# Turning and spreading k's column maxima on VectorE instead of TensorE, for twenty of thirty-two units

## The chip, the cores and the metric

The kernel runs on one core of a Trainium2 chip. A core has a matrix engine (TensorE, PE in the profile; its weight loads are PEld), VectorE (DVE), ScalarE (ACT), GpSimd (POOL), and SyncE (SP), which here issues most of the DMAs. Each engine works through its own queue in order; engines wait for one another by semaphores. On-chip memory is SBUF and, for the results of TensorE, PSUM; both have 128 partitions. The metric is the device time of one execution in microseconds, as the median of several.

## What is computed

An attention without a score matrix, and a mixing network behind it. All inputs are fp32:

```python
def _attn_ref(q, k, v):  # each (8, 8, 576, 64)
    q_s = q - np.max(q, axis=-1, keepdims=True)
    q_s = np.exp(q_s)
    q_s = q_s / (np.sum(q_s, axis=-1, keepdims=True) + 1e-09)
    k_s = k - np.max(k, axis=2, keepdims=True)
    k_s = np.exp(k_s)
    k_s = k_s / (np.sum(k_s, axis=2, keepdims=True) + 1e-09)
    kv = np.einsum('bhsd,bhse->bhde', k_s, v)
    return np.einsum('bhsd,bhde->bhse', q_s, kv)
...
    xt = x.transpose(0, 2, 1)  # x: the heads joined, (8, 576, 512)
    h = np.maximum(xt @ w_tok1, 0.0) @ w_tok2
    u = x + h.transpose(0, 2, 1)
    h2 = np.maximum(u @ w_ch1, 0.0) @ w_ch2
    return u + h2
```

The part that matters here is the softmax of k: it runs over the sequence (axis 2), so each of the 64 columns of a head has one maximum over 576 rows.

## The kernel before

The work on the attention is cut into 32 **units**, each a batch entry and a pair of heads: 128 columns (two heads of 64), 576 rows in five blocks of 128 (the last 64 rows stand twice, which changes no maximum). The network behind it is cut into nine **groups** of 512 rows. A group has twelve **steps**; a step is `ch1` (line 402: twelve matmuls of 512 columns into one PSUM bank `ps_h`, then a rectifier that splits the result into a high part `h2h` on ScalarE, line 412, and a low part `h2l` on VectorE, line 413) and, one step later, `ch2` (line 417: twelve matmuls that add to the four banks `ps_o`, line 421). The products use fp32r operands in pairs of high and low parts; a few small products use plain fp32. After a group's last step `out_end` (line 438) adds the input to the output on VectorE (lines 452 and 453) and stores it.

The first eight units (`early`) are worked before the steps begin. Units 8 to 31 are woven into the steps by the list `todo` (lines 551 to 583): units 8 to 11 two steps apart, units 12 to 31 three steps apart. For a unit n from 12 on come at its step `stage_kv(n)` (the product of k and v, line 277), `stage_y(n)`, `stage_qT(n)` and `soft(n + 1)`, then the loads of unit n + 2, `stage_h1(n)` and, at the next unit, `stage_u(n)`. This is the order in which the program is written; the order in each engine's queue is laid out by Tile when the program is built (line 666), which moves an instruction ahead where its inputs are ready. So an instruction of one unit may run some units ahead.

`soft(n)` is `softmax_k` (line 216) and `softmax_q` (line 240). Both k and its transpose `kt` are loaded, so that the maxima can be had by a reduce along the free axis: line 219 reduces `kt` (128 columns on the partitions, 640 rows along the free axis, 64 of them twice) to `mc`, one number for each partition. But k itself lies with the rows on the partitions and the columns along the free axis, so the 128 maxima must be turned from a column into a row, and the row must be on all partitions. For the units from the ninth on this goes in three steps: ScalarE multiplies the identity by `mc` into `dg`, a diagonal matrix (line 233); TensorE multiplies a matrix of ones by it, which puts the row of the maxima on every partition of a PSUM bank (line 235); ScalarE copies that to `mb` in SBUF (line 236). GpSimd subtracts `mb` from k (line 237), ScalarE takes the exponential (line 238), and a later `stage_kv` reads it.

`dg` and `mb` are one buffer each, for all units; `mc` has two; `kt` has one and k two. `ps_unit` (line 119) hands out the PSUM banks of `ps_h` in turn, four of them, shared with `ch1`.

`stage_qT` (line 296) turns q on VectorE in a similar way to what the change does: a transpose of 32x32 blocks (line 315), then copies of the blocks to their places (line 323), two of three on VectorE and one on ScalarE. GpSimd's other operation in a unit is the low part of q, line 115, in `split`.

Of the kernel before, what the change touches and what calls it, by code (L numbers as in the profile page):

```python
# [8 lines left out]
F32 = mybir.dt.float32  # L9
F32R = mybir.dt.float32r  # L10
U32 = mybir.dt.uint32
AF = mybir.ActivationFunctionType
# [3 lines left out]
P = 128  # L16
# [4 lines left out]
def attn_mixer_kernel(ctx: ExitStack, tc: tile.TileContext, q, k, kt, v, wt, out, dims):  # L21
# [3 lines left out]
    nc = tc.nc  # L25
    B, H, S, D, TOK, DM, DCH, wide = dims
    NJ = DM // P
# [8 lines left out]
    NE = 2 * NJ  # L36
# [6 lines left out]
    sm = ctx.enter_context(tc.tile_pool(name="sm", bufs=2))  # L43
# [6 lines left out]
    ident = const.tile([P, P], F32R, name="ident")  # L50
# [11 lines left out]
    ones = const.tile([P, P], F32, name="ones")  # L62
# [26 lines left out]
    dg = lay.tile([P, P], F32, name="dg")  # L89
    for i in range(3):  # L90
        slots[i][1] = lay.tile([P, NJ, CW], F32R, name=f"ul{i}")
    mb = lay.tile([P, P], F32, name="mb")
# [14 lines left out]
    Q = 32  # L107

    def f32(ap):
        return ap.bitcast(F32)  # L110
# [8 lines left out]
    def ps_unit(dtype=F32):  # L119

        pools = unit_banks[0]
        pool, name = pools[turn[0] % len(pools)]
        turn[0] += 1
        return pool.tile([P, 512], dtype, name=name)
# [90 lines left out]

    def softmax_k(u):
        ktt = u["kt"]
        mc = sm.tile([P, 1], F32, name="mc")
        nc.vector.tensor_reduce(mc, ktt, axis=AX.X, op=ALU.max)  # L219
        kx = u["k"]  # L220
        if u["early"]:
            nc.vector.tensor_scalar(mc, mc, -1.0, None, op0=ALU.mult)
            nc.scalar.activation(ktt, ktt, AF.Exp, bias=mc)
            t = ps_unit()
            for c in range(C):
                nc.tensor.transpose(t[:, c * P : (c + 1) * P], ktt[:, c * P : (c + 1) * P], f32(ident))
            nc.scalar.copy(kx[:, 0:C, :], t.rearrange("p (c d) -> p c d", c=C))
            t = ps_unit()
            turned_k.append(nc.tensor.transpose(t[:, 0:P], ktt[:, S0 : S0 + P], f32(ident)).ins)
            nc.scalar.copy(kx[:, C, :], t[:, 0:P])  # L230
            return

        nc.scalar.activation(dg, f32(ident), AF.Copy, scale=mc)  # L233
        t = ps_unit()
        nc.tensor.matmul(t[:, 0:P], ones, dg, start=True, stop=True)  # L235
        nc.scalar.copy(mb, t[:, 0:P])  # L236
        nc.gpsimd.tensor_tensor(kx, kx, mb.unsqueeze(1).broadcast_to([P, C1, P]), op=ALU.subtract)  # L237
        nc.scalar.activation(kx, kx, AF.Exp)

# [223 lines left out]
    def soft(n):  # L463
        if n < NU:
            softmax_k(units[n])
            softmax_q(units[n])
# [204 lines left out]
```

## Time and profile before

| | us |
|---|---|
| median of three runs | 818.27 (816.95 to 819.36) |
| the profiled execution | 817.88 |
| its span, from the first to the last instruction | 816.1 |
| TensorE busy in the span | 797.1 |
| VectorE busy | 486.7 |
| ScalarE busy | 342.2 |
| GpSimd busy | 83.6 |
| line 235, TensorE busy, 48 matmuls in 24 units | 9.4 |
| mean TensorE clock granted | 0.992 of full speed |

How to read the rows that follow. A row of a group has the line, the engine, the operation, what it writes and reads, the shape of one and the number of them; behind the first bar the busy time in all and the mean of one in ns; behind the second the idle time of the engine just before them, and what ended it. A row of the timeline has the start, the time from the first start to the last end of the instructions merged in it, and the instruction; a bracket shows idle time of the engine before it and its releaser. A row of the windows has the stretch, its length, and for each engine the busy time with the number of instructions. Matmuls overlap: the one behind starts before the one ahead has ended, so their cost is read from start to start.

### The profile page before, as it was taken

The numbers are of one execution on the slowest core, as the hardware profiler recorded it, in microseconds if no ns is written. First come the engines' busy times: TensorE is split into PE (matmuls) and PEld (weight loads), VectorE is DVE, ScalarE is ACT, GpSimd is POOL, SyncE is SP. The second block draws the span as 40 slices with busy tenths as digits, with TensorE's granted clock in tenths as the row PEclk, the third lists the DMA queues.
The fourth block names the chain that finished last, engine by engine and source line by source line (L and its number), as shares of the span: only waits on it lengthen the run. The fifth ranks groups of instructions, "written<-read, shape, count | busy, mean of one in ns | idle before, by whom it ended". The sixth has DMA issues, their size and how long they took to land.

```text
span 816.1 us, 11997 instructions
## 1 busy us (share of the span) xinstructions
PE 797.1 (98%) x4512; PEld 677.0 (83%) x4512; DVE 486.7 (60%) x1104; ACT 342.2 (42%) x898; POOL 83.6 (10%) x69
## 2 busy tenths in 40 slices
PE   7799999989999999999999999999999999999997
PEld 5688888878888888888888888888888888888886
DVE  6999998887876555755576555755575314113112
ACT  6977564448553334343444444443443321101110
POOL 1000010102121100111111111111011100000200
PEclk8999999999999999999999999999999999999999
DMA  9752433414223111322232222312121001001001
GB/s 298 245 162 93 149 110 109 145 65 124 86 63 115 52 30 53 110 61 64 63 100 79 64 64 63 113 51 63 26 87 35 15 1 51 1 1 52 1 1 51
DMA packets 60633, 63.55 MB, mean 78 GB/s; under 512 B 40864, under 2 KB 40992, under 8 KB 60576
## 3 DMA queue, kind: packets, MB, share of 16 engines
q1 hardware_dynamic: 55392, 53.36, 21.8%
q10 hardware_dynamic: 5184, 9.44, 3.1%
q8 instruction: 35, 0.57, 0.3%
q14 instruction: 22, 0.18, 0.1%
HBM read 53.35 MB, written 9.44 MB: 77 GB/s over the span
## 4 chain that ended last, share of the span: by engine, by line
PE 89%; DVE 6%; DMA 3%; ACT 1%; issue 1%; DVEq 0%; ACTq 0%
PE ps_h L409 34%; PE ps_o L421 34%; PE ps_h L381 8%; PE ps_h L337 6%; PE ps_h L277 2%; DMA stg<-in_w 2%; PE ps_h L345 1%; PE ps_o L381 1%; DVE mc L219 1%; PE ps_h L235 1%; DVE cv_s L176 1%; DVE q_t L323 1%; DMA q_t<-in_q 1%; DVE st L245 1%; ACT q_t L251 1%
## 5 line engine op out<-in xcount | busy, mean ns | idle before, releaser
L409 PE MATMUL ps_h<-uh,cw 128*128 128x512 f32 x864 | 269.7, 392 | 0.6 <-DVE cw L115 0.6
L421 PE MATMUL ps_o<-h2h,cw 128*128 128x512 f32 x864 | 263.4, 394 | 2.2 <-DVE cw L115 2.2
L421 PEld LDWEIGHTS ps_o<-h2h,cw 128*128 128x128 f32 x864 | 160.6, 189 | 34.3 <-ACT h2h L412 2.4
L409 PEld LDWEIGHTS ps_h<-uh,cw 128*128 128x128 f32 x864 | 160.3, 188 | 33.2 <-DVE cw L115 1.0
L412 ACT ACTIVATE h2h<-ps_h 128x512 fp32r<-128x512 f32 x108 | 64.5, 597 | 292.8 <-PE ps_h L409 276.6
L413 DVE SCALAR_TENSOR_TENSOR h2l<-ps_h,h2h 128x512 fp32r<-128x512 f32 x108 | 74.0, 685 | 187.3 <-ACT h2h L412 186.9
L409 PE MATMUL ps_h<-ul,cw 128*128 128x512 f32 x432 | 168.2, 389 | 0.0
L421 PE MATMUL ps_o<-h2l,cw 128*128 128x512 f32 x432 | 161.7, 392 | 0.0
L421 PEld LDWEIGHTS ps_o<-h2l,cw 128*128 128x128 f32 x432 | 81.4, 189 | 16.8
L409 PEld LDWEIGHTS ps_h<-ul,cw 128*128 128x128 f32 x432 | 81.1, 188 | 17.0
L115 POOL TENSOR_TENSOR ql<-q_t,qh 128x640 fp32r<-128x640 f32 x24 | 39.3, 1636 | 484.8 <-ACT qh L114 406.3
L323 DVE COPY q_t<-cv_s 32x160 f32<-32x160 f32 (+1 forms) x264 | 65.8, 249 | 6.3 <-POOL ql L115 3.0
L245 DVE TENSOR_REDUCE st<-q_t 128x10 f32<-128x640 f32 x32 | 26.2, 818 | 41.8 <-DMA q_t<-in_q 41.8
L237 POOL TENSOR_TENSOR k_t<-k_t,mb 128x640 f32<-128x640 f32 x24 | 38.0, 1582 | 73.8 <-ACT mb L236 73.8
L323 ACT COPY q_t<-cv_s 32x128 f32<-32x128 f32 (+1 forms) x120 | 36.8, 307 | 2.1 <-DVE cv_s L315 0.7
L219 DVE TENSOR_REDUCE mc<-kt_t 128x1 f32<-128x640 f32 x32 | 26.0, 812 | 14.7 <-ACT dg L233 12.4
L381 PE MATMUL ps_h<-w2h,hh 128*128 128x320 f32 (+1 forms) x112 | 33.4, 299 | 0.0
L256 ACT ACTIVATE q_t<-q_t 128x640 f32<-128x640 f32 x24 | 17.8, 741 | 36.4 <-DVE q_t L255 36.4
L381 PE MATMUL ps_h<-w2l,hh 128*128 128x320 f32 (+1 forms) x112 | 33.0, 296 | 0.0
L381 PE MATMUL ps_h<-w2h,hl 128*128 128x320 f32 (+1 forms) x112 | 32.7, 298 | 0.0
L388 ACT CAST uh<-ps_h 128x320 fp32r<-128x320 f32 (+4 forms) x76 | 25.4, 336 | 15.1 <-PE ps_h L381 11.8
L389 DVE TENSOR_TENSOR ul<-ps_h,uh 128x320 fp32r<-128x320 f32 (+4 forms) x76 | 27.2, 373 | 4.0 <-ACT uh L388 3.1
(144 smaller groups left out, 1061.9 us busy)
## 6 DMA issues: line engine op xcount, KB each, us to landing
stg<-in_w SPq DMA_DIRECT2D x28, 512.0 KB, 4.1
kt_t<-in_kt SPq DMA_DIRECT2D x32, 320.0 KB, 3.1
q_t<-in_q SPq DMA_DIRECT2D x32, 320.0 KB, 3.3
v_t<-in_v SPq DMA_DIRECT2D x64, 128.0 KB, 2.8
out<-stg ACTq DMA_DIRECT2D x32, 256.0 KB, 2.1
k_t<-in_k SPq DMA_DIRECT2D x24, 320.0 KB, 3.5
v_t<-in_v SPq DMA_DIRECT2D x32, 32.0 KB, 2.7
out<-part ACTq DMA_DIRECT2D x4, 256.0 KB, 2.0
```

What stands on the lines that cost most here:

```text
L115: lo_eng.tensor_tensor(lo, src, f32(hi), op=ALU.subtract)
L219: nc.vector.tensor_reduce(mc, ktt, axis=AX.X, op=ALU.max)
L237: nc.gpsimd.tensor_tensor(kx, kx, mb.unsqueeze(1).broadcast_to([P, C1, P]), op=ALU.subtract)
L245: nc.vector.tensor_reduce(st[:, 0, :], qt, axis=AX.X, op=ALU.max)
L323: eng(qx[ys, 0:n, xs], turned[xs, 0:n, ys])
L337: nc.tensor.matmul(y[:, 0:TOK], a, w, start=(i == 0), stop=(i == len(mm) - 1))
L381: nc.tensor.matmul(t[:, 0:N], a, w, start=(i == 0), stop=(i == len(mm) - 1))
L389: nc.vector.tensor_tensor(ul, src, f32(uh), op=ALU.subtract).ins,
L409: nc.tensor.matmul(t, cw[f][x][:, n, :], w, start=(i == 0), stop=(i == 3 * NJ - 1))
L412: nc.scalar.activation(hh, t, AF.Relu).ins,
L413: nc.vector.scalar_tensor_tensor(hl, t, 0.0, f32(hh), op0=ALU.max, op1=ALU.subtract).ins,
L421: nc.tensor.matmul(o, cw[f][x][:, n, :], w, start=(first and i == 0), stop=(last and i == 2))
```

## The change

For units 12 to 31 (`NE + NJ` is 12) VectorE does the turn and the copying itself. The reduce writes the maxima into the first column of `dg` (in place of `mc`). A transpose of 32x32 blocks, which reads that one column 32 times, puts into columns 32 to 63 of `dg` on each group of 32 partitions the row of that group's 32 maxima, the same on all 32 partitions. Sixteen copies then take these 32x32 squares to their places: four column positions of `mb`, each on four groups of partitions. The multiplication by the identity, the product with ones and the copy from PSUM are left out for these units. Units 8 to 11 keep the old way.

```diff
     def softmax_k(u):
         ktt = u["kt"]
-        mc = sm.tile([P, 1], F32, name="mc")
+        through = u["n"] >= NE + NJ
+        mc = dg[:, 0:1] if through else sm.tile([P, 1], F32, name="mc")
         nc.vector.tensor_reduce(mc, ktt, axis=AX.X, op=ALU.max)
...
-        nc.scalar.activation(dg, f32(ident), AF.Copy, scale=mc)
-        t = ps_unit()
-        nc.tensor.matmul(t[:, 0:P], ones, dg, start=True, stop=True)
-        nc.scalar.copy(mb, t[:, 0:P])
+        if through:
+
+            nc.vector.transpose(dg[:, Q : 2 * Q], mc.broadcast_to([P, Q]))
+            for x in range(P // Q):
+                for y in range(P // Q):
+                    nc.vector.tensor_copy(
+                        mb[y * Q : (y + 1) * Q, x * Q : (x + 1) * Q], dg[x * Q : (x + 1) * Q, Q : 2 * Q]
+                    )
+        else:
+            nc.scalar.activation(dg, f32(ident), AF.Copy, scale=mc)
+            t = ps_unit()
+            nc.tensor.matmul(t[:, 0:P], ones, dg, start=True, stop=True)
+            nc.scalar.copy(mb, t[:, 0:P])
         nc.gpsimd.tensor_tensor(kx, kx, mb.unsqueeze(1).broadcast_to([P, C1, P]), op=ALU.subtract)
```

## The prediction

> **What bounds the kernel now.** I read the head of the page first, then its slices, then the busy time by stages, then single rows of the timeline. The engine lines of the page and three of its slice rows:
>
> ```profile
> span 816.1 us, 11997 instructions
> PE 797.1 (98%) x4512; PEld 677.0 (83%) x4512; DVE 486.7 (60%) x1104; ACT 342.2 (42%) x898; POOL 83.6 (10%) x69
> PE   7799999989999999999999999999999999999997
> DVE  6999998887876555755576555755575314113112
> PEclk8999999999999999999999999999999999999999
> ```
>
> TensorE is busy nearly everywhere, at full clock from the second slice on. Busy is no proof that it is the bound, since matmuls overlap; the stage in which the change acts has to be looked at alone. The twenty units that change have their TensorE turns (line 235) between 216 and 640 us, so I asked for the busy time of each engine in that stage, and for one period of it (from the k-v product of one unit at 410.7 to that of the next at 432.7):
>
> ```profile
> core 0: us, PE busy (x) PEld busy (x) DVE busy (x) ACT busy (x) POOL busy (x), PEclk, DMA share, GB/s
> 216.00:640.00 424.00, 424.00 (x2506) 363.89 (x2503) 258.10 (x614) 183.57 (x444) 62.11 (x40) 1.00 0.23 69
> 410.70:432.70 22.00, 22.00 (x132) 18.89 (x132) 16.67 (x38) 9.40 (x23) 3.10 (x2) 1.00 0.35 107
> ```
>
> TensorE has no idle time at all in those 424 us, VectorE is busy for 61% of them, ScalarE for 43%, GpSimd for 15%. So a TensorE instruction that disappears here brings the end forward by the time from its start to the next one's, and anything else pays only if TensorE comes to wait for it. The period shown holds the four output additions of a finished group as well, and VectorE has only 5.3 us left in it.
>
> **What is removed, on TensorE.** Rows of the timeline around one line 235, in order of start:
>
> ```profile
> 413.19 0.38 PE L235 MATMUL ps_h<-dg,ones 128*128 128x128 f32 x2
> 413.33 0.71 PE L421 MATMUL ps_o<-h2h,cw 128*128 128x512 f32 x2
> 413.88 0.39 PE L421 MATMUL ps_o<-h2l,cw 128*128 128x512 f32 x1
> 414.11 0.62 PE L421 MATMUL ps_o<-h2h,cw 128*128 128x512 f32 x2
> 414.57 0.40 PE L421 MATMUL ps_o<-h2l,cw 128*128 128x512 f32 x1
> ```
>
> One fp32 product of the source is two matmuls in the trace. Two matmuls of line 421 take 414.57 - 414.11 = 0.46 us from start to start. From 413.19 to 413.88 run the pair of line 235 and two matmuls of line 421: 0.69 us. The pair costs 0.69 - 0.46 = 0.23 us: 0.14 of its own and 0.09 by which the two that follow it are late. With twenty pairs this is 20 x 0.23 = **4.6 us**. The bounds: 20 x 0.14 = 2.8 us if those that follow stay late behind another fp32 product, and 20 x 0.24 = 4.8 us by rounding. I take 4.6, since in the row above the line 235 pair stands between fp32r products on both sides. Each pair also held a PSUM bank (ps_h) for a time; with TensorE never waiting, I cost its return at nothing.
>
> **What is removed elsewhere.** The groups by line:
>
> ```profile
> L233 ACT ACTIVATE dg<-ident,mc 128x128 f32<-128x128 f32 x24 | 9.8, 408 | 0.2
> L236 ACT COPY mb<-ps_h 128x128 f32<-128x128 f32 x24 | 6.4, 265 | 9.4 <-PE ps_h L235 9.3
> L219 DVE TENSOR_REDUCE mc<-kt_t 128x1 f32<-128x640 f32 x32 | 26.0, 812 | 14.7 <-ACT dg L233 12.4 <-DMA kt_t<-in_kt 2.3
> ```
>
> ScalarE loses 20 x (0.408 + 0.265) = 13.5 us, and its in-order waits for line 235. VectorE's reduce no longer waits for ScalarE's read of an older mc (12.4 us in nine times). Neither engine bounds the stage, so both are worth 0, and that is hidden behind TensorE's 424 of 424.
>
> **What is added, on VectorE.** Per unit one transpose of 32 columns and sixteen copies of 32x32. The trace has neither, so the nearest rows:
>
> ```profile
> L323 DVE COPY q_t<-cv_s 32x160 f32<-32x160 f32 x144 | 39.5, 274 | 4.7 <-POOL ql L115 3.0
> L323 DVE COPY q_t<-cv_s 32x128 f32<-32x128 f32 x120 | 26.3, 219 | 1.6
> L315 DVE STREAM_TRANSPOSE cv_s<-q_t 128x640 f32<-128x640 f32 x24 | 20.1, 839 | 0.3
> L282 DVE TENSOR_SCALAR rs<-ps_h 128x1 f32<-128x1 f32 x27 | 4.0, 150 | 0.1
> ```
>
> The copies of line 323 also move 32-partition blocks from one group of partitions to another, with four or five times the columns. From above, sixteen at 0.22 us and a transpose of at most 0.84 give 4.4 us a unit. From below, a one-column operation lasts 0.15, so 16 x 0.15 + 0.15 = 2.6 us if they follow one another without overlap; if each could start before the one ahead has ended, less. I take 0.18 for a copy and 0.25 for the transpose, nearer to line 323 than to the one-column row: 16 x 0.18 + 0.25 = **3.1 us a unit**, 62 us over twenty. VectorE then has 258 + 62 = 320 of 424 us (75%), and 16.7 + 3.1 = 19.8 of 22 in the full period above. It stays under TensorE, so this costs nothing as long as no product of VectorE comes late.
>
> [...]
>
> **Who waits for VectorE.** The queue of VectorE is in order. The copies wait until GpSimd's subtraction (line 237) of the unit before has read mb. Behind them may stand the h2l of line 413, for which TensorE waits two steps later, and the output additions of 452 and 453. The tightest of them in the period shown:
>
> ```profile
> 413.15 0.29 DVE L115 TENSOR_TENSOR kvl<-kvf,kvh 128x128 fp32r<-128x128 f32 x1 [1.09 <-ACT kvh L114]
> 414.89 0.82 DVE L219 TENSOR_REDUCE mc<-kt_t 128x1 f32<-128x640 f32 x1 [1.44 <-ACT dg L233]
> 416.57 0.82 DVE L245 TENSOR_REDUCE st<-q_t 128x10 f32<-128x640 f32 x1 [0.86 <-DMA q_t<-in_q]
> 421.58 0.68 DVE L413 SCALAR_TENSOR_TENSOR h2l<-ps_h,h2h 128x512 fp32r<-128x512 f32 x1
> ...
> 425.24 0.39 PE L421 MATMUL ps_o<-h2l,cw 128*128 128x512 f32 x1
> ```
>
> That h2l ends at 421.58 + 0.68 = 422.26 and is first read at 425.24: a **slack of 3.0 us**. Ahead of it VectorE has idle pieces of 1.44 and 0.86, together 2.3 us. So even if all 3.1 us stood ahead of this one instruction, it would come 3.1 - 2.3 = 0.8 us late, within the slack. This cover, 5.3 us, is what hides the added work.
>
> The path of k itself has more room. GpSimd's subtraction and the product that needs it, one unit:
>
> ```profile
> 416.05 1.56 POOL L237 TENSOR_TENSOR k_t<-k_t,mb 128x640 f32<-128x640 f32 x1
> 418.04 0.74 ACT L238 ACTIVATE k_t<-k_t 128x640 f32<-128x640 f32 x1
> 432.69 0.80 PE L277 MATMUL ps_h<-v_t,k_t 128*64 128x65 f32 x20
> ```
>
> From the end of the exponential (418.78) to the product lie 13.9 us. Maxima now share dg with their turned form, a single buffer, so the reduce of a unit has to stand behind the transpose of the unit before, and the reload of kt's single buffer (SP's queue) behind that reduce. These reduces ran far ahead, as the first and last starts of the two lines show:
>
> ```profile
> L219 DVE TENSOR_REDUCE mc<-kt_t x32: 762/814/822, 3.9 to 571.2; 128x1 f32<-128x640 f32 x32
> L235 PE MATMUL ps_h<-dg,ones x48: 270/273/377, 145.7 to 635.2; 128*128 128x128 f32 x48
> ```
>
> The last unit's maxima are there 64 us before TensorE turns them. Some of that lead goes; I cost it at nothing, with the 13.9 us as cover. No DMA is added or taken away.
>
> **The sum.** The profiled execution took 817.9 us (span 816.1): 817.9 - 4.6 = 813.3. The median of the three runs is 818.3, so 818.3 - 4.6 = **813.7 us**. About 0.3% (2.5 us) is what a measurement of this kernel can tell from no change.
>
> **Rivals.**
>
> *The copies wait for GpSimd, in part of the units.* For this speaks a stretch where VectorE's copies met line 237:
>
> ```profile
> 636.44 4.08 DVE L323 COPY q_t<-cv_s 32x160 f32<-32x160 f32 x11 [2.43 <-POOL ql L115]
> 636.37 1.57 POOL L237 TENSOR_TENSOR k_t<-k_t,mb 128x640 f32<-128x640 f32 x1
> ```
>
> By the means of 0.274 and 0.219 eleven such copies take about 11 x 0.25 = 2.8 us; here they took 4.08, 1.3 more, and GpSimd worked until 637.94. GpSimd has two operations of 1.57 in a period, 3.1 us. If the sixteen copies run into both, the added block is 3.1 + 3.1 = 6.2 us against a cover of 5.3: TensorE waits 0.9 us. If this happens only in the periods with output additions, one in four, it costs 5 x 0.9 = 4.5 us: 813.7 + 4.5 = 818.2, no change. [...] Against the rival: GpSimd is active for 15% of the stage only, and the order of each queue, laid out when the program is built, can put small copies into gaps. Chance 0.24.
>
> *VectorE becomes the bound, in all units.* Same place (h2l ahead of line 421), decided once block plus wait exceeds 5.3 us plus the gain of 0.23 in every period. With the middle price and both GpSimd operations each unit loses 0.9 us, 20 x 0.9 = 18 us: 813.7 + 18 = 832 us. With the upper price of 4.4 it is 2.2 a unit, 858 us. For it speaks the full period, where 16.7 + 6.2 exceeds 22; against it that VectorE keeps 424 - 320 = 104 us of the stage idle, 5.2 for each unit. Chance 0.16.
>
> *The freed time is not won.* If other fp32 products move next to where line 235 stood, or the changed queue order inserts waits of its own, half of the gain or less is left: 813.7 + 2.8 = 816.5. Against it: the order of TensorE was stall-free with and around the pair. Chance 0.05.
>
> *Forecast*: the copies lie in VectorE's gaps. Chance 0.55; its own range is 812 to 815.5.
>
> **How the numbers follow.** The range reaches from 811.8 (4.8 us won, and 1.7 for the spread of the runs, 816.95 to 819.36) to 820.6, which takes in the forecast, the freed time not won and most of the partial wait; what it leaves out is the bound on VectorE and its edges. Faster by over 0.3% (under 815.8): the forecast and a little of the partial waits, 0.58. Within 0.3%: most of the partial waits and the freed time not won, 0.24. Slower: 0.18.
>
> **What would show it.** Right: TensorE loses the 40 matmuls of line 235 in 216 to 640 us, is still busy throughout there, and a period shrinks from 22.0 to about 21.8 us. VectorE rises to about three quarters of the stage, each copy at 0.15 to 0.22 us. Wrong: rows of TensorE that name h2l (line 413 before) or kvl as releaser, copies of over 1 us beside line 237, or waits of VectorE for k_t of GpSimd in front of h2l; then the cover was too thin and the time is that of the second or third case.

## The result, and the profile after

| | before | after |
|---|---|---|
| median of six runs each, us | 817.51 (816.93 to 819.36) | 858.98 (857.54 to 864.37) |
| ratio after / before, 95% interval | | 1.0518 (1.0494 to 1.0542) |
| the profiled execution, its span, us | 817.88, 816.1 | 857.93, 856.1 |
| TensorE busy, us; matmuls | 797.1; 4512 | 802.3; 4472 |
| VectorE busy, us | 486.7 | 559.6 |

The forecast was 813.7; the kernel became 41.5 us slower. The head of the page of the kernel after, and two of its slice rows:

```profile
span 856.1 us, 12196 instructions
...
PE 802.3 (94%) x4472; PEld 674.1 (79%) x4472; DVE 559.6 (65%) x1444; ACT 327.6 (38%) x858; POOL 83.7 (10%) x69
...
PE   7799999989899999999999999899999999999997
...
DVE  6999998868887677786668666966767424113112
```

The 40 matmuls are gone, as intended, and TensorE is nevertheless busy for 5 us more; one reason is its granted clock, which is 0.50 from 221.0 to 227.8 us, in and behind a wait of 4.23 us that ended at 222.4 (the last section shows another such place). The stage of the twenty units, and one period of it (from the first `ch1` matmul of a step to that of the third step behind it), in the windows:

```profile
core 0: us, PE busy (x) PEld busy (x) DVE busy (x) ACT busy (x) POOL busy (x), PEclk, DMA share, GB/s
216.00:664.00 448.00, 416.38 (x2404) 350.08 (x2403) 325.76 (x926) 165.13 (x396) 59.54 (x38) 0.99 0.22 65
393.61:416.71 23.10, 22.08 (x130) 18.58 (x129) 15.97 (x46) 8.66 (x20) 3.12 (x3) 1.00 0.18 50
```

Before, TensorE was busy for 424.00 of 424.00 us here. Now the stage has 448, TensorE stands idle in 31.6 of them, and this period takes 23.10 us instead of 22.0. VectorE is busy for 73% of the stage, close to the 75% that the sum gave it: it is not full, and still TensorE waits for it. The groups that carry this (busy time, mean ns of one, then idle time ahead and its releaser), first three of the kernel before:

```profile
L421 PE MATMUL ps_o<-h2l,cw 128*128 128x512 f32 x432 | 161.7, 392 | 0.0
...
L323 DVE COPY q_t<-cv_s 32x160 f32<-32x160 f32 (+1 forms) x264 | 65.8, 249 | 6.3 <-POOL ql L115 3.0
...
L237 POOL TENSOR_TENSOR k_t<-k_t,mb 128x640 f32<-128x640 f32 x24 | 38.0, 1582 | 73.8 <-ACT mb L236 73.8
```

and of the kernel after:

```profile
L431 PE MATMUL ps_o<-h2l,cw 128*128 128x512 f32 x432 | 162.6, 397 | 17.4 <-DVE h2l L423 17.4
...
L333 DVE COPY q_t<-cv_s 32x160 f32<-32x160 f32 (+1 forms) x264 | 85.4, 323 | 6.9 <-POOL ql L115 3.6
...
L239 DVE COPY mb<-dg 32x32 f32<-32x32 f32 x320 | 57.7, 180 | 4.1
...
L247 POOL TENSOR_TENSOR k_t<-k_t,mb 128x640 f32<-128x640 f32 x24 | 38.0, 1582 | 113.6 <-ACT mb L246 63.8 <-DMA k_t<-in_k 45.1 <-DVE mb L239 4.8
```

The first row after answers the question of the prediction: these matmuls wait 17.4 us for h2l, and 0.0 before. A new copy (line 239) lasts 0.180 us, just what was taken. But the old copies of q (line 333, line 323 before) have grown from 249 to 323 ns, 19.6 us in all, though the change does not touch them. And GpSimd's subtraction (line 247) now waits 45.1 us for the load of k. TensorE also waits for the output additions, which the prediction named as well, once for each of four groups, where it didn't before:

```profile
PE ps_o L431 <- DVE stg L462: 6.9, 4, 2.1
```

One period in the timeline, in order of start:

```profile
394.22 0.82 DVE L255 TENSOR_REDUCE st<-q_t 128x10 f32<-128x640 f32 x1 [3.13 <-DMA q_t<-in_q]
394.95 4.13 DVE L333 COPY q_t<-cv_s 32x160 f32<-32x160 f32 x11
...
395.19 1.56 POOL L247 TENSOR_TENSOR k_t<-k_t,mb 128x640 f32<-128x640 f32 x1 [1.45 <-DMA k_t<-in_k]
...
396.10 0.39 PE L419 MATMUL ps_h<-ul,cw 128*128 128x512 f32 x1
...
399.11 0.83 DVE L265 TENSOR_TENSOR q_t<-q_t,st 128x640 f32<-128x640 f32 x1
...
399.86 2.96 DVE L239 COPY mb<-dg 32x32 f32<-32x32 f32 x16
...
399.97 0.74 ACT L266 ACTIVATE q_t<-q_t 128x640 f32<-128x640 f32 x1 [2.45 <-DVE q_t L265]
...
400.62 0.58 ACT L422 ACTIVATE h2h<-ps_h 128x512 fp32r<-128x512 f32 x1
...
403.58 0.68 DVE L423 SCALAR_TENSOR_TENSOR h2l<-ps_h,h2h 128x512 fp32r<-128x512 f32 x1
...
404.31 0.73 PE L431 MATMUL ps_o<-h2l,cw 128*128 128x512 f32 x2 [1.02 <-DVE h2l L423]
```

Read it from the bottom. The last matmul of `ch1` (396.10) ends at 396.49, and its h2l starts only at 403.58, 7.1 us later. Three things stand in front of it on VectorE. The first is a wait of 3.13 us for the load of q, with nothing moved into it. The second is eleven copies of line 333 in 4.13 us instead of the 2.7 of most units before: GpSimd's subtraction starts 0.24 us behind the first of them. The third is the sixteen new copies, 2.96 us. ScalarE comes late as well: its queue has the exponential of q (line 266) in front of h2h (line 422), and that exponential waits for VectorE's line 265. Before, in the same place, the two stood the other way round:

```profile
419.09 0.60 ACT L412 ACTIVATE h2h<-ps_h 128x512 fp32r<-128x512 f32 x1 [0.31 <-PE ps_h L409]
...
421.10 0.74 ACT L256 ACTIVATE q_t<-q_t 128x640 f32<-128x640 f32 x1 [1.41 <-DVE q_t L255]
```

Nobody wrote this exchange: the order of each queue is laid out when the program is built, and the change laid it out anew for all engines.

To see where the time is lost I took the start of each step's first `ch1` matmul and subtracted the same of the kernel before (profiled executions; units 14 to 31 lie in steps 24 to 78, three steps to a unit, and behind step 78 nothing changes). The last two columns are medians over every third step from 30 on, where h2l is tightest (30 to 75): the time from the end of `ch1` to the start of h2h, and from the end of h2l to its first read.

| us later than before at step | 15 | 24 | 33 | 48 | 63 | 78 | h2h late | slack of h2l |
|---|---|---|---|---|---|---|---|---|
| before | | | | | | | 0.04 | 3.0 |
| after | +0.2 | +11.3 | +16.4 | +24.1 | +33.4 | +39.6 | 4.56 | 0.06 |
| e1, no copies | -1.0 | +1.5 | +11.1 | +10.1 | +9.3 | +8.6 | 4.32 | 0.47 |
| e2, half of the copies | +0.4 | +6.7 | +7.5 | +8.3 | +10.2 | +11.9 | 4.55 | 0.17 |
| e3, before plus the copies | -0.7 | -1.2 | +5.5 | +7.6 | +9.2 | +9.2 | 0.04 | 1.93 |
| e4, copies pinned behind h2l | -0.3 | +8.0 | +7.4 | +7.3 | +9.8 | +10.1 | 3.09 | 1.77 |
| e5, subtraction behind ql | 0.0 | +10.9 | +11.1 | +14.2 | +18.7 | +20.3 | 3.56 | 0.06 |
| e6, e4 from unit 14 on | -0.9 | -1.6 | -2.3 | -1.7 | +0.3 | +0.3 | 3.09 | 1.92 |
| e7, product in fp32r | +2.2 | +7.0 | +6.5 | +6.1 | +5.5 | +4.8 | | |
| e8, maxima through DRAM | +93.7 | +148.7 | +148.1 | +147.1 | +145.9 | +144.6 | | |
| e9, e8 from unit 14 on | +0.6 | +13.7 | +16.0 | +16.3 | +19.3 | +18.7 | | |
| e10, e6 less four units | -1.2 | +0.1 | -0.5 | -1.1 | -2.0 | -3.1 | 3.06 | 1.5 |

The kernel after loses 11 us before step 24, and then 39.6 - 16.4 = 23.2 us in the fifteen units from step 33 to 78, 1.55 each. The early loss has a place of its own:

```profile
206.87 2.96 DVE L239 COPY mb<-dg 32x32 f32<-32x32 f32 x16
...
213.05 1.96 POOL L115 TENSOR_TENSOR ql<-q_t,qh 128x640 fp32r<-128x640 f32 x1 [1.52 <-issue]
...
213.62 3.66 DVE L239 COPY mb<-dg 32x32 f32<-32x32 f32 x13
...
217.29 0.84 DVE L325 STREAM_TRANSPOSE cv_s<-q_t 128x640 f32<-128x640 f32 x1
...
221.98 0.38 DVE L363 SCALAR_TENSOR_TENSOR hl<-ps_h,hh 128x256 fp32r<-128x256 f32 x1
...
222.41 0.64 PE L391 MATMUL ps_h<-w2h,hl 128*128 128x320 f32 x1 [4.23 <-DVE hl L363]
```

The new maxima live in dg, and dg is in use for unit 11's product in the old way, whose last matmul (line 245) starts at 202.5 us. The reduces of the units behind it are held back till then, and the transposes, reduces and copies of units 12 and 13 come in a bunch. TensorE waits 4.23 us for an hl that stands behind them.

### The profile page after: what moved, and what is told of

Same layout as the page of the kernel before. It is cut to its first block, busy times and chain, and to the rows that moved or that the text cites. A ratio compares the mean times of both kernels' runs of the same rounds, so it can differ in the third digit from the quotient of the medians.

```text
span 856.1 us, 12196 instructions
## 1 busy us (share of the span) xinstructions
PE 802.3 (94%) x4472; PEld 674.1 (79%) x4472; DVE 559.6 (65%) x1444; ACT 327.6 (38%) x858; POOL 83.7 (10%) x69
## 4 chain that ended last, share of the span: by engine, by line
PE 51%; DVE 31%; DMA 11%; issue 2%; ACT 2%; SPq 2%; POOL 0%; DVEq 0%; ACTq 0%; POOLq 0%
PE ps_h L419 19%; PE ps_o L431 18%; DVE q_t L333 9%; DMA q_t<-in_q 8%; DVE mb L239 7%; PE ps_h L391 6%; PE ps_h L347 4%; DVE st L255 2%; DVE h2l L423 2%; DVE q_t L265 2%; PE ps_h L287 2%; DMA stg<-in_w 2%; DVE st L267 2%; DMA kt_t<-in_kt 1%; SPq L155 1%
## 5 line engine op out<-in xcount | busy, mean ns | idle before, releaser
L431 PE MATMUL ps_o<-h2h,cw 128*128 128x512 f32 x864 | 260.6, 392 | 12.7 <-DVE stg L462 6.9
L431 PE MATMUL ps_o<-h2l,cw 128*128 128x512 f32 x432 | 162.6, 397 | 17.4 <-DVE h2l L423 17.4
L423 DVE SCALAR_TENSOR_TENSOR h2l<-ps_h,h2h 128x512 fp32r<-128x512 f32 x108 | 73.3, 679 | 147.1 <-ACT h2h L422 147.1
L431 PEld LDWEIGHTS ps_o<-h2l,cw 128*128 128x128 f32 x432 | 80.5, 189 | 39.6 <-DVE h2l L423 23.4
L333 DVE COPY q_t<-cv_s 32x160 f32<-32x160 f32 (+1 forms) x264 | 85.4, 323 | 6.9 <-POOL ql L115 3.6
L239 DVE COPY mb<-dg 32x32 f32<-32x32 f32 x320 | 57.7, 180 | 4.1
L347 PE MATMUL ps_h<-w1h,qh 128*128 128x256 f32 x96 | 29.1, 303 | 2.0 <-DVE h2l L423 2.0
```

The source lines that it names most:

```text
L239: nc.vector.tensor_copy(mb[y * Q : (y + 1) * Q, x * Q : (x + 1) * Q], dg[x * Q : (x + 1) * Q, Q : 2 * Q])
L333: eng(qx[ys, 0:n, xs], turned[xs, 0:n, ys])
L347: nc.tensor.matmul(y[:, 0:TOK], a, w, start=(i == 0), stop=(i == len(mm) - 1))
L423: nc.vector.scalar_tensor_tensor(hl, t, 0.0, f32(hh), op0=ALU.max, op1=ALU.subtract).ins,
L431: nc.tensor.matmul(o, cw[f][x][:, n, :], w, start=(first and i == 0), stop=(last and i == 2))
```

## The experiments

Four causes had to be told apart: that VectorE simply has too much to do; that the copies stand ahead of h2l with less cover than was counted; that copies are held by GpSimd's operations; and that the loss is in what the change sets free in the queues' order, whatever the copies cost. In the letters of the first expectations A is that the copies and the wait of the old copies for GpSimd add up against the slack of h2l, B the copies in front of h2l alone, C that wait for GpSimd alone, and D VectorE's total load.

**e1, no copies.** The kernel after without the sixteen copies of units 12 to 31; an older unit's row of maxima is subtracted instead.

```diff
-            for x in range(P // Q):
-                for y in range(P // Q):
-                    nc.vector.tensor_copy(
...
```

> Leaves out the sixteen copies for units 12 to 31, so that k is reduced by an old row of maxima; all else as in the changed kernel, and GpSimd's subtraction still runs one unit ahead, beside line 333's copies. Theory A (the copies, 2.96 us, and the wait of line 333's copies for GpSimd, 1.3 us, add up against a slack of about 3.0 us): 1.3 is under 3.0, no waits of TensorE, about 813 us. Theory B (the copies in front of h2l alone): about 813 us. Theory C (the wait for GpSimd alone): little changes, 845 to 859 us. Theory D (VectorE's total load): about 813 us.

Measured: 829.31 us (826.46 to 830.05), ratio 1.0136 (1.0113 to 1.0159), between what the theories gave. Rows of one period:

```profile
406.12 4.00 DVE L328 COPY q_t<-cv_s 32x160 f32<-32x160 f32 x11
406.21 1.57 POOL L242 TENSOR_TENSOR k_t<-k_t,mb 128x640 f32<-128x640 f32 x1 [1.62 <-DMA k_t<-in_k]
...
411.65 0.58 ACT L417 ACTIVATE h2h<-ps_h 128x512 fp32r<-128x512 f32 x1
```

Without one new copy, the subtraction still meets the copies of q (17 of these last over 0.7 us; before 2, after 18), and h2h is still 4.3 us late. So the reordering doesn't come from the copies. But it costs nothing in the middle of the stage: from step 33 to 78 this kernel gains 2.5 us on the one before. Its loss of about 10 lies in steps 24 to 33, where TensorE waits 2.8 us for an output addition and three times for h2l, 0.3, 1.8 and 3.0 us; from 255 to 300 us, where the last two of these lie, the mean granted clock is 0.96 (1.00 in the kernel before). This loss belongs to an order that e1 has for itself. The reduces and transposes of all twenty units have run by 289 us here (after: by 618), and the h2l behind which TensorE waits 3.0 us stands behind two reduces that wait 1.2 and 2.7 us for the load of kt. So from step 33 on VectorE has not only no copies but also 1.0 us less of reduce and transpose in a unit, and e1 leaves out more than the copies.

**e2, half of the copies.** Two of the four blocks for each column group; half of the partitions keep an older unit's maxima.

```diff
-                for y in range(P // Q):
+                for y in range(2):
```

> Leaves out eight of the sixteen copies, so that half of the partitions keep an old row of maxima. Theory A: 1.5 + 1.3 = 2.8 us against 3.0, waits nearly gone, 813 to 818 us. Theory B, in proportion: half of the loss, about 836 us. Theory C: 845 to 859 us. Theory D: half of the loss, about 836 us.

Measured: 827.01 us (826.05 to 829.82), ratio 1.012 (1.0097 to 1.0143). Half of the copies take away 32 of 41.5 us, and from step 33 to 78 only 4.4 us are lost instead of 23.2. The loss is not proportional to the copies: there is a threshold, as a cover has one.

**e3, before plus the copies.** The kernel before, with line 235 and everything around it; for units 14 to 31 VectorE also does the transpose and sixteen copies, into a place that nobody reads.

```diff
+        if u["n"] >= NE + NJ + 2:
+            spare = part[:, 3, :]
+            nc.vector.transpose(spare[:, P : P + Q], mc.broadcast_to([P, Q]))
...
+                        spare[y * Q : (y + 1) * Q, x * Q : (x + 1) * Q], spare[x * Q : (x + 1) * Q, P : P + Q]
```

> The kernel before with the transpose and the sixteen copies added on VectorE for units 14 to 31, into space that nobody reads; TensorE keeps its products, and GpSimd's subtraction stays right behind its other operation as before. The copies stand in front of h2l as in the changed kernel. Theory A: 2.96 against 3.0 us, 818 to 826 us. Theory B: 18 of 20 units lose what the changed kernel loses, 818 + 41 = about 859 us. Theory C: about 818 us. Theory D: 855 to 862 us.

Measured: 828.5 us (826.59 to 830.16), ratio 1.0132 (1.0106 to 1.0158). Rows of one period:

```profile
404.43 0.60 ACT L420 ACTIVATE h2h<-ps_h 128x512 fp32r<-128x512 f32 x1 [0.31 <-PE ps_h L417]
...
406.92 2.96 DVE L238 COPY part<-part 32x32 f32<-32x32 f32 x16
...
409.91 0.69 DVE L421 SCALAR_TENSOR_TENSOR h2l<-ps_h,h2h 128x512 fp32r<-128x512 f32 x1
```

Here h2h is on time, and the copies stand in front of h2l. From step 33 to 78 this costs 3.7 us, 0.25 a unit. So there the prediction's cover does hide the added work, nearly, in the order for which it was read off. From step 24 to 33 e3 loses 6.7 us. The place that nobody reads is a part of the tile `part`, and the first transpose waits there for the store of `part` (till 252.3 us); those of the next three units follow at 256.3, 261.4 and 272.4, later ones some 22 us apart. In this bunch TensorE waits 1.55 and 2.64 us for an h2l behind copies. Copies alone 0.25, reordering alone -0.17, both together 1.55 a unit: the two use up the same cover. (e3 keeps the pairs of line 235 and e1 does not, which is 0.23 of the difference between the first two.)

**e5, the subtraction behind ql.** The kernel after, with one constraint: GpSimd's subtraction stands behind the ql of the same unit, as it did before.

```diff
+                with tc.issue_after(units[n]["ql_ins"]):
+                    subtract_k(units[n])
```

> The changed kernel with one constraint: GpSimd's subtraction of a unit's maxima stands right behind the low part of the same unit's q (as it did before the change), no longer one unit ahead, where it waited for the load of k and met line 333's copies. VectorE's queue has the same order as in the changed kernel, the sixteen copies in front of h2l. If the wait for GpSimd and the copies are both needed to use up the slack (3.3 us in the middle of the stage), units 14 to 31 lose next to nothing and only the loss of 7 to 11 us at the first units stays: 824 to 832 us. If the copies alone do it: 850 to 859 us.

Measured: 838.97 us (838.09 to 840.99), ratio 1.0262 (1.0248 to 1.0276), between the two ranges given. Its groups:

```profile
L435 PE MATMUL ps_o<-h2l,cw 128*128 128x512 f32 x432 | 161.3, 394 | 4.5 <-DVE h2l L427 4.4
L337 DVE COPY q_t<-cv_s 32x160 f32<-32x160 f32 (+1 forms) x264 | 71.9, 272 | 7.7 <-POOL ql L279 4.5
```

The subtraction no longer waits for k's load, the copies of q are back from 323 to 272 ns, and TensorE's wait for h2l falls from 17.4 to 4.4 us. That the subtraction runs a unit ahead thus costs 859.0 - 839.0 = 20.0 us, in the presence of the copies. The rest stays: the copies still stand in front of h2l, whose slack is 0.06.

**e4, the copies pinned behind h2l.** From unit 14 on, copies and subtraction are placed one step later, behind the h2l of that step, so that they can delay no h2l ahead of it.

```diff
+    def late_spread(n):
+        if NE + NJ + 2 <= n < NU:
+            with behind(drained):
+                spread_k(units[n])
...
+        put(at + 1, lambda n=n: late_spread(n + 1))
```

> The changed kernel with the same work, but for units 14 to 31 the sixteen copies and GpSimd's subtraction stand one step later in the program and behind that step's h2l in VectorE's queue. Theory A and B: nothing stands in front of h2l, 813 to 817 us. Theory C: the subtraction no longer meets line 333's copies, 813 to 817 us. Theory D: the load is the same, 850 to 859 us.

**e6, the same, and the old way up to unit 13.** Units 12 and 13 keep line 235's product, so that dg passes from the old way to the new later, behind the crowded stretch.

```diff
-        through = u["n"] >= NE + NJ
+        through = u["n"] >= NE + NJ + 2
```

> As the run with the copies behind h2l, but the new way begins with unit 14 instead of 12, so that its first reduce does not have to wait for dg in the crowded stretch from 185 to 240 us. If the 8 us lost there come from the first two units' work bunched behind the old use of dg: 819 to 823 us. If the loss comes with whichever unit is the first: 827 to 831 us.

Measured: e4 829.29 us (828.51 to 831.23), ratio 1.015 (1.013 to 1.017); e6 821.4 us (818.16 to 823.2), ratio 1.0051 (1.0033 to 1.007). In e4 no copy of q is long any more and the slack of h2l is 1.77. VectorE's work is that of the kernel after, so its total (theory D, 850 to 859 us) is not the cause. What is left of the loss lies mostly before step 24 (+8.0), and e6 takes that away (-1.6 there). Of TensorE's waits (for whom: us in all, times, longest), the two largest for VectorE that the kernel before does not have, in e4:

```profile
PE ps_h L353 <- DVE h2l L429: 4.8, 4, 1.5
PE ps_h L397 <- DVE hl L369: 4.2, 1, 4.2
```

In e6 the first row is the same, 4.8 us in four waits. The 4.2 for hl is gone; four waits of up to 1.5 us stay in both. In e6 they come at 344.8, 433.7, 522.2 and 610.7 us, each some 8 us behind the output additions of a group. In the other periods e6 gains 0.2 us a unit.

**e10, e6 less those four.** Units whose copies would fall in a period with output additions keep line 235's product.

```diff
-        through = u["n"] >= NE + NJ + 2
+        through = u["n"] >= NE + NJ + 2 and u["n"] % NJ != 1
```

> As the run that begins with unit 14 and has the copies behind h2l, but the four units whose copies fall into a period with output additions keep the product. If these periods are what is left of the loss (1.3 to 1.5 us each, four of them) while each other unit wins 0.23 us: 821.4 - 4 x 1.4 + 4 x 0.23, less 0.9 for the four pairs that stay, 815 to 817 us. If the copies cost something in every unit: 820 to 822 us.

Measured, in twelve runs: **814.9 us** (813.12 to 816.28), ratio 0.9967 (0.9954 to 0.998), 0.3% faster than the kernel before. One period:

```profile
395.46 2.71 DVE L339 COPY q_t<-cv_s 32x160 f32<-32x160 f32 x11
...
399.71 0.58 ACT L428 ACTIVATE h2h<-ps_h 128x512 fp32r<-128x512 f32 x1
...
400.57 0.68 DVE L429 SCALAR_TENSOR_TENSOR h2l<-ps_h,h2h 128x512 fp32r<-128x512 f32 x1
...
401.17 2.95 DVE L250 COPY mb<-dg 32x32 f32<-32x32 f32 x16
...
402.13 0.39 PE L437 MATMUL ps_o<-h2l,cw 128*128 128x512 f32 x1
```

The copies of q take 2.71 us again, h2l ends at 401.25 and is read at 402.13 without a wait, the sixteen copies follow it, and the subtraction starts when they are done (404.20), far from the copies of q. Though h2h is still about 3 us late, the 2.95 us are now where nobody waits for them.

Three further runs asked what a pair of line 235 is worth by itself.

**e7, the product in fp32r.** The kernel before, with dg and the matrix of ones as fp32r, which is to make one matmul of two: a product of line 421, in fp32r, is one matmul in the kernel before (1296 in 108 steps of twelve).

```diff
-    dg = lay.tile([P, P], F32, name="dg")
+    dg = lay.tile([P, P], F32R, name="dg")
```

> The kernel before, with the ones and the diagonal matrix of the maxima as fp32r (line 235), so that the product is one matmul with fp32r neighbours; VectorE gets nothing in the units. A row of maxima rounded to fp32r gives the same softmax but for rounding, since the row cancels. If a pair costs 0.23 us of which 0.09 is the change between fp32 and fp32r: 24 x (0.23 - 0.06) = 4 us less, 813 to 814.5 us. If an fp32r product of 128 columns is as long as the pair: 817 to 818 us.

Measured: 822.5 us (818.98 to 823.57), ratio 1.0052 (1.0037 to 1.0067). From step 24 to 78 it gains 2.2 us, 0.12 a unit, half of a pair's 0.23; but it is 7 us late by step 18, before any of that. The kernel has one more copy at the start; that this laid out the queues in another order is likely and not shown.

**e8 and e9, the maxima through DRAM.** Two small DMAs in SP's queue carry the maxima to DRAM and back to all partitions, for units 8 to 31 (e8) or 14 to 31 (e9); no product, no copies.

```diff
+        nc.sync.dma_start(mrow[u["n"]], mc)
+        nc.sync.dma_start(mb, mrow[u["n"]].rearrange("p o -> o p").broadcast_to([P, P]))
```

> The kernel before, but for units 8 to 31 the maxima go by a DMA of 128 x 4 bytes to DRAM and by a second one back as a row on all partitions; no product, no ScalarE copies, no VectorE copies; the subtraction stands behind the low part of the same unit's q. If TensorE is the bound and nothing else comes late, 24 x 0.23 = 5.4 us less: 811.5 to 813.5 us. If the two DMAs hold up SP's loads of q and k: over 818 us.

> As the run through DRAM, but only for units 14 to 31 (the others keep the product) and with two slots in DRAM in place of one for each unit, so that the small stores no longer stand in SP's queue among the loads of the weights. If a removed pair is worth 0.23 us and nothing else comes late: 18 x 0.23 = 4.1 us less, about 813.8 us. If the small DMAs hold up the loads of q and k: over 818 us.

Measured: e8 964.26 us (961.68 to 965.38), ratio 1.1787 (1.1768 to 1.1805); e9 836.67 us (835.96 to 838.92), ratio 1.024 (1.0217 to 1.0263). In e8, the start and a part of the stage:

```profile
200.00:330.00 130.00, 63.62 (x281) 50.99 (x281) 53.22 (x118) 30.23 (x94) 6.14 (x4) 0.72 0.65 68
600.00:700.00 100.00, 100.00 (x599) 85.77 (x598) 56.79 (x146) 41.70 (x102) 15.46 (x10) 1.00 0.21 62
```

and among its waits:

```profile
DVE mc L219 <- DMA kt_t<-in_kt: 151.4, 26, 9.0
```

The DMAs that carry the maxima stand in the same queue as the loads, and VectorE waits 151.4 us for kt (2.3 in the kernel before), all of it ahead of step 24, where e8 is 148.7 us late. That loads stood behind a DMA which waited for a maximum is my reading of this; no row here shows it by itself. After that TensorE is full, and from step 33 to 78 e8 gains 148.1 - 144.6 = 3.5 us, 0.23 for each of fifteen units: the price of a pair where nothing else is in the way. e9 loses the same way, in steps 19 to 21 above all (+0.5 to +13.7). VectorE waits 6.9 and 4.8 us for kt there, and TensorE 5.5 us for an h2l and 3.2 us for an hl behind these waits. From 267 us on, behind that loss, the next reduce also waits for the maxima's own store. The two rows:

```profile
DVE mc L219 <- DMA mrow<-mc: 53.3, 14, 5.2
...
DVE mc L219 <- DMA kt_t<-in_kt: 13.8, 4, 6.9
```

## Why the prediction was wrong

**Right.** TensorE was the bound; each removed pair is worth 0.23 us where nothing waits (e8); a copy lasts 0.180 us, for which 0.18 was taken; the block of copies and transpose is 2.96 + 0.20 us, for which 3.1 was taken; VectorE has 73% of the stage, for which 75% was given. The sum took the copies one behind another, without overlap. So they came: a block of sixteen in 2.96 us is 0.185 from start to start, and a copy lasts 0.180.

**Wrong: the cover.** The step that failed is "even if all 3.1 us stood ahead of this one instruction, it would come 3.1 - 2.3 = 0.8 us late, within the slack", and with it the cover of 5.3 us. The 3.0 us of slack and the idle pieces were rightly read off, in one period of the kernel before (over the sixteen from step 30 to 75 its slack runs from 1.9 to 3.6 us); e3 shows from step 33 on that they nearly suffice there. The prediction took them over into a kernel whose queues are laid out anew. In the kernel after h2h starts 4.56 us behind `ch1` instead of 0.04, so most of the slack is gone before VectorE has begun; the idle piece ahead of h2l is a wait for q's load (3.13 us) that no copy was put into; and the copies of q take 1.3 us longer. e1 and e2 show the cover that is left: 0.47 without copies, 0.17 with half of them, 0.06 and TensorE waiting with all.

**Wrong: "the path of k itself has more room", at nothing.** It had 13.9 us of room, and the new layout used it: the subtraction came one unit ahead, where it waits for k's load and then runs beside the copies of q. Of these 18 start within 0.25 us of a line 247 and last 1.49 to 1.66 us instead of about 0.25, some 1.3 us more each, 23 us in all. Taking most of this away gave 20.0 us back (e5, where seven long copies are left). The mechanism was named, in the rival "the copies wait for GpSimd": there it was the new copies that were to meet GpSimd, in one period of four. It was the old copies, in nearly every unit. Each of the 18 ends 0.11 us behind the end of the subtraction beside it, which takes 1.55 to 1.63 us. That GpSimd's two operations add their whole 3.1 us to a block, as the rivals took it, no run shows; one subtraction added some 1.3 us to a copy that met it.

**Wrong: dg, "Some of that lead goes; I cost it at nothing".** For the last units that holds. With units 12 and 13 in the new way four reduces and 32 copies stand bunched between 202 and 224 us, and e6 shows what these two units cost: 829.3 - 821.4 = 7.9 us. That the wait for dg made the bunch is read off the rows. In e6 dg is shared too, from unit 14 on, without such a loss, so sharing it costs this only in the crowded stretch.

The loss in parts, each the difference of two kernels; the right column is the difference of their profiled executions at step 78, since the runs of e6 spread over 5 us:

| | medians, us | profiled, us |
|---|---|---|
| subtraction a unit ahead, beside the copies of q (after to e5) | 20.0 | 19.3 |
| copies in front of h2l; the subtraction moves with them (e5 to e4) | 9.7 | 10.2 |
| units 12 and 13 in the new way, with dg shared (e4 to e6) | 7.9 | 9.8 |
| copies in the periods with output additions (e6 to e10) | 6.5 | 3.4 |
| left to the good (before to e10) | -2.6 to -2.9 | -3.1 |

Since two of these use the same cover, their shares depend on the order in which they are taken away; and 10.9 - 8.0 = 2.9 us of the second row's 10.2 lie before step 24. What is left to the good agrees with the 14 pairs that e10 removes: 14 x 0.23 = 3.2 us.

Of the rivals the second, "VectorE becomes the bound, in all units", named the place (h2l ahead of line 421) and, with its upper price, 858 us. The number is right by accident: the price of a block was 3.2 us and not 4.4, and VectorE was not full. Its chance of 0.16 was too low for a case in which three changes (the copies, the path of k, dg) were costed at nothing, two of them on the same cover. The range ended at 820.6, since the partial waits were the only slower case let into it. Of the signs that were to show the cover too thin, two came: TensorE's waits for h2l, and copies of over 1 us beside GpSimd's subtraction.

Not settled: why the laid-out order puts the exponential of q in front of h2h. In the steps of the two last columns it does so, with h2h some 3 us late or more, in most periods of every kernel that takes line 235's product away (after, e1, e2, e4 to e6, e8 to e10). But the product alone does not decide it: e7, which keeps one, has this order in the first seven of the sixteen periods (0.7 to 1.3 us late), and the kernel before and e3 have it in the periods at steps 72 and 75 (2.6 and 2.7 us late). In e8 and e9 h2h is as late, and nothing is lost by that in the middle of e8's stage, where there are no copies.

## What to carry to other kernels

A slack read off a profile belongs to the order in which that profile ran; where a build lays out the queues anew, an edit that frees an instruction (here the subtraction) can move it onto something that was clear of it, so ask of each freed instruction where it may run and what it will hold up there. Put work that has time to spare behind the instruction that hasn't, by a stated order, instead of trusting gaps; with the same sixteen copies a unit the change cost 41.5 us, and gained 2.6 once copies and subtraction stood behind h2l and the six units in crowded places kept the old way. Two small costs that are each hidden by the same cover must be added before they are compared with it.

## What was unexpected in the hardware

Behind some of its longer waits TensorE lost time a second time, by its clock. In e3, behind a wait of 2.64 us, the matmuls came 0.43 us apart instead of 0.23, and the windows show the granted clock there and behind it:

```profile
274.50 0.80 PE L429 MATMUL ps_o<-h2l,cw 128*128 128x512 f32 x1 [2.64 <-DVE h2l L421]
275.09 1.06 PE L429 MATMUL ps_o<-h2h,cw 128*128 128x512 f32 x2
275.94 0.63 PE L429 MATMUL ps_o<-h2l,cw 128*128 128x512 f32 x1
```

```profile
274.50:277.40 2.90, 2.90 (x7) 2.34 (x8) 2.70 (x13) 0.00 (x0) 0.00 (x0) 0.50 0.00 0
278.00:281.00 3.00, 3.00 (x15) 2.47 (x14) 2.13 (x3) 0.00 (x0) 0.00 (x0) 1.00 0.00 0
```

At half the clock seven matmuls lose some 1.5 us more, without any idle time in the profile. Behind the wait of 1.82 us in e1 one interval was 0.34 and the next ones 0.24. In the kernel before the granted clock is 0.50 from 171.9 to 175.2 us, behind a wait of 2.18 us that ended at 171.1. It did not come behind every wait of about this length: one of 2.13 us in the kernel after, which ended at 545.7, left the clock at 1.00.

Copies are not all that lasted longer beside GpSimd: in e10 a multiply of two tiles in SBUF (line 276), whose mean in the kernel after is 0.82 us (line 270 there), began 0.61 us behind the start of a subtraction of 1.57 and took 1.64:

```profile
404.20 1.57 POOL L253 TENSOR_TENSOR k_t<-k_t,mb 128x640 f32<-128x640 f32 x1 [11.01 <-DVE mb L250]
...
404.81 1.64 DVE L276 TENSOR_TENSOR q_t<-q_t,st 128x640 f32<-128x640 f32 x1
```
